# Shared row-sum products, 128-key leftover scores, ten filler products and a new written-out order in a sparse-attention plus rational-MLP kernel

## The chip, the core and the metric

The kernel runs on one NeuronCore of a Trainium2 chip. A core has a matrix engine (PE, with its weight loads shown as PEld), a vector engine (DVE), an activation engine (ACT), a general engine (POOL), and a sync engine (SP) that here only starts transfers. Each engine executes its own instruction list in order; they meet through semaphores. Transfers started from SP and from POOL are carried by the same 16 DMA engines. The metric is the device time of one execution in microseconds; the kernel before took 363.92 us as the median of nine runs (361.21 to 365.72).

## The reference

For 8 batches, 8 heads, 576 positions and head size 64, attention is computed with two masks, and its result goes through a two-layer network with a rational activation:

```python
scores = scale * np.matmul(q, k.transpose(0, 1, 3, 2))
mask_local = (rel >= 0) & (rel < 32)                               # heads 0..3
mask_strided = (rel >= 0) & (pos[None, :] % 32 == pos[:, None] % 32)  # heads 4..7
attn = softmax(np.where(mask, scores, -1e9)); attn_out = np.matmul(attn, v)
x = attn_out.transpose(0, 2, 1, 3).reshape(4608, 512)
h = x @ w_in                                    # 512 -> 2048
g = (a0 + a1*h + a2*h**2 + a3*h**3) / (1 + |b0||h| + |b1|h**2 + 1e-6)
out = g @ w_out                                 # 2048 -> 512
```

## The kernel before

**Stages.** The work is cut into 8 batches of attention and 9 chunks of 512 rows for the network: chunk c < 8 is the first 512 positions of batch c, chunk 8 collects the 64 leftover positions of all batches. For a batch b, `loads(b)` starts the transfers of q, k and v; `scores(b)` makes transposed copies and scores; `attend(b, ...)` makes five output tiles T0 to T4 (T4 is the leftover one); `dense1(c)` is the first layer with the activation; `dense2(c)` the second layer and the store.

**Scores.** R1 transposes the strided heads' k and q on PE into `sT` (for b < TB = 4; later batches use a DMA transpose, step T). R2 and R3 do the same for the local heads (`kL`, `qL`). S and L are the strided and the local scores, each followed by an exponential on ACT into `ES` and `EL`. TL is a DMA transpose of the leftover rows (`tm` to `LT`), X the leftover scores (into `EX`, `EW`). Masks are added by products of `IDN` and `MK`.

**Attend.** A tile is a set of small products into one PSUM pair: 16 local ones (`EL` times `VL`) and 8 strided ones (`ES` times v). For b = 1, 2, 3 (VSB = 4) the strided v lies without a column of ones, so each strided product has a second one with one column, against `ONE`, for the row sum. DVE then takes the reciprocal of the sums (L877) and multiplies (L879) into one of three buffers `XR`; the transpose of `XR` into `XT` is done on PE for b < 2 and by a DMA transpose from SP (L909) after that. Since there are three `XR` buffers, tile n+3 can be written only when the transpose of tile n has been read out: in batch 2, T3 uses the buffer of T0.

**Network.** `dense1` makes eight pairs of 4 x 2 products of 512 columns per chunk (written below as D1.c.f0, f2, ... f14), copied by ACT into `HB` (L975). DVE and ACT evaluate the rational function in steps called d1 to d9 in the code (L989 to L1040; the logarithm and the exponential that make the reciprocal are on ACT, L1013 and L1016). Chunk 0 is cut into groups of 2, 2, 4 and 8 slices, chunk 1 into 4, 4 and 8, so that DVE can begin early. `dense2` is 4 x 8 products for each of two halves (D2.c).

**Order.** Every operation gets a rank from the list `ORDER`, in the sequence in which the program adds operations; each engine's instruction list is its operations sorted by rank. So `ORDER` alone says what stands before what on PE, DVE, ACT, and on the two queues of transfers, SP and POOL. `fill` is a set of NF0 = 20 products of 128 x 512 whose results are not used; they stand on PE among the first operations. The POOL transfers that carry `hw0` wait for the fourth q/k transfer of batch 0 (the q of heads 0 to 3). The transfers of batch b's q and k wait until the transposes of batch b-1 have read their buffers, and those of v until the tiles of the batch before have been computed.

Of the kernel before, what the change touches and what calls it, by code (L numbers as in the profile page):

```python
# [7 lines left out]
BF = dt.bfloat16  # L8
F32 = dt.float32
# [6 lines left out]
def _bf16_bits(x):  # L16
# [7 lines left out]
    5, 7, 13, 9, 15, 103, 38, 43, 45, 55, 20, 46, 171, 85, 2, 0, 42, 68, 79, 63, 61, 69, 65, 82, 70, 59, 76,  # L24
    97, 29, 62, 22, 24, 99, 23, 106, 32, 57, 4, 19, 6, 21, 11, 36, 10, 26, 16, 18, 12, 8, 17, 14, 56, 72,
    66, 51, 37, 110, 141, 145, 30, 41, 44, 49, 50, 33, 52, 35, 27, 28, 54, 87, 90, 71, 80, 96, 100, 25, 31,
    39, 48, 34, 40, 47, 64, 53, 58, 75, 78, 81, 89, 101, 83, 88, 91, 94, 98, 86, 93, 95, 102, 111, 104, 108,
    109, 112, 114, 77, 116, 120, 123, 125, 128, 133, 135, 168, 60, 73, 92, 107, 118, 124, 127, 130, 139,
    136, 117, 132, 121, 126, 84, 74, 105, 67, 131, 137, 3, 1, 192, 198, 182, 173, 113, 138, 140, 143, 144,
    148, 164, 169, 153, 157, 122, 129, 142, 146, 150, 152, 159, 154, 156, 160, 163, 172, 174, 115, 119, 134,  # L30
    147, 151, 183, 187, 158, 161, 166, 170, 208, 215, 167, 176, 155, 165, 185, 188, 191, 224, 234, 195, 201,
    211, 254, 277, 282, 190, 197, 181, 193, 205, 213, 196, 204, 222, 236, 244, 288, 297, 257, 303, 262, 269,
    291, 298, 317, 322, 175, 179, 180, 203, 207, 178, 184, 199, 219, 221, 220, 226, 227, 230, 241, 212, 217,
    218, 223, 246, 162, 209, 216, 233, 231, 240, 253, 260, 263, 149, 186, 194, 202, 239, 235, 200, 245, 247,
    252, 232, 249, 243, 238, 189, 210, 177, 206, 256, 259, 214, 255, 268, 258, 265, 261, 279, 225, 229, 237,
    242, 248, 251, 264, 271, 274, 278, 275, 311, 319, 321, 324, 283, 286, 287, 290, 292, 295, 296, 300, 299,
    304, 305, 308, 307, 315, 316, 318, 329, 369, 375, 384, 250, 266, 267, 273, 281, 289, 306, 313, 327, 314,
    320, 336, 357, 361, 365, 285, 294, 280, 284, 310, 333, 339, 378, 402, 343, 348, 387, 395, 401, 418, 301,
    323, 293, 309, 325, 331, 312, 326, 351, 370, 377, 412, 421, 429, 446, 383, 389, 451, 456, 461, 466, 272,
    228, 276, 270, 347, 344, 350, 338, 349, 341, 353, 355, 342, 302, 332, 335, 360, 359, 382, 379, 367, 364,  # L40
    427, 431, 424, 434, 328, 330, 334, 337, 352, 358, 362, 368, 373, 385, 372, 393, 399, 441, 439, 396, 406,
    407, 411, 420, 425, 426, 430, 432, 435, 438, 444, 442, 449, 450, 453, 462, 489, 492, 496, 340, 346, 345,
    354, 356, 363, 366, 374, 376, 381, 380, 388, 386, 391, 390, 397, 409, 428, 440, 482, 537, 464, 504, 473,
    477, 565, 574, 519, 550, 455, 486, 494, 516, 525, 546, 553, 585, 405, 413, 422, 433, 443, 457, 507, 447,
    454, 459, 467, 472, 531, 509, 371, 394, 404, 436, 410, 417, 392, 400, 414, 415, 419, 398, 423, 408, 468,
    469, 475, 465, 505, 501, 471, 479, 488, 487, 483, 481, 474, 485, 506, 524, 534, 520, 518, 416, 403, 437,
    458, 445, 452, 463, 476, 490, 499, 511, 517, 460, 498, 521, 529, 528, 539, 542, 544, 555, 547, 558, 559,
    570, 564, 569, 571, 575, 573, 581, 583, 586, 589, 601, 602, 605, 470, 480, 484, 491, 503, 512, 532, 543,
    523, 533, 540, 548, 551, 557, 549, 554, 560, 572, 577, 582, 608, 651, 660, 590, 595, 673, 692, 634, 700,
    594, 604, 611, 627, 637, 657, 667, 706, 478, 495, 515, 556, 563, 567, 628, 568, 576, 579, 584, 588, 672,  # L50
    631, 448, 514, 530, 538, 500, 493, 527, 502, 536, 497, 508, 510, 522, 513, 593, 597, 599, 600, 622, 624,
    633, 614, 616, 629, 621, 620, 618, 625, 606, 654, 649, 655, 535, 526, 545, 541, 562, 578, 587, 591, 603,
    617, 623, 630, 552, 580, 638, 648, 646, 662, 664, 665, 668, 669, 674, 675, 677, 680, 684, 685, 689, 688,
    693, 694, 697, 702, 731, 733, 758, 607, 615, 619, 626, 632, 643, 656, 666, 650, 658, 663, 670, 676, 682,
    671, 678, 687, 696, 701, 728, 746, 772, 785, 713, 717, 801, 813, 760, 790, 708, 726, 735, 752, 763, 783,
    792, 822, 592, 598, 613, 641, 686, 766, 764, 691, 698, 703, 709, 718, 820, 810, 561, 566, 652, 659, 640,
    610, 635, 644, 612, 645, 596, 639, 636, 609, 707, 710, 712, 704, 737, 734, 724, 716, 736, 732, 721, 740,
    727, 729, 771, 774, 745, 770, 681, 647, 642, 653, 683, 690, 695, 699, 720, 725, 738, 742, 661, 705, 748,
    753, 757, 775, 779, 780, 784, 786, 789, 791, 805, 794, 798, 799, 803, 804, 808, 814, 816, 824, 864, 871,
    874, 714, 722, 730, 739, 743, 754, 768, 778, 761, 769, 776, 781, 787, 796, 782, 797, 802, 809, 815, 823,  # L60
    870, 858, 877, 830, 834, 885, 901, 897, 905, 832, 840, 845, 865, 873, 881, 887, 916, 723, 750, 795, 800,
    807, 859, 891, 812, 818, 827, 841, 850, 863, 919, 747, 679, 755, 749, 741, 765, 744, 711, 762, 767, 756,
    759, 715, 719, 829, 826, 835, 831, 856, 853, 842, 848, 839, 851, 849, 837, 838, 844, 857, 855, 861, 862,
    773, 777, 751, 793, 806, 811, 817, 821, 825, 828, 833, 846, 788, 819, 852, 866, 868, 878, 880, 886, 889,
    892, 895, 896, 911, 899, 902, 906, 908, 909, 912, 915, 917, 921, 924, 951, 954, 836, 843, 847, 854, 860,
    869, 875, 882, 872, 876, 879, 883, 888, 893, 884, 890, 898, 903, 907, 926, 941, 922, 929, 925, 927, 937,
    962, 946, 953, 914, 931, 934, 940, 944, 952, 960, 965, 867, 894, 900, 904, 910, 957, 920, 913, 918, 923,
    928, 935, 956, 961, 930, 933, 936, 939, 942, 945, 932, 948, 947, 950, 955, 959, 963, 967, 958, 964, 970,
    975, 977, 996, 1002, 986, 1000, 980, 983, 1018, 1022, 1005, 1015, 981, 985, 988, 999, 1003, 1009, 1016,
    1027, 938, 943, 949, 966, 969, 974, 971, 978, 982, 984, 987, 991, 995, 993, 968, 973, 976, 979, 990,  # L70
    994, 972, 989, 997, 1021, 1023, 1040, 1047, 1033, 1037, 1032, 1036, 1042, 1046, 1053, 1058, 1006, 1008,
    1025, 1030, 1035, 1039, 1043, 1050, 1057, 1051, 1055, 1060, 1063, 1067, 1071, 1044, 1054, 1062, 1066,
    1069, 1072, 1079, 1074, 1078, 1085, 1090, 1094, 1097, 1007, 1011, 1019, 1077, 1082, 1086, 1091, 1088,
    1092, 1095, 1098, 1100, 1102, 992, 998, 1001, 1004, 1010, 1013, 1014, 1012, 1017, 1020, 1024, 1026,
    1031, 1028, 1029, 1034, 1038, 1041, 1045, 1048, 1083, 1049, 1052, 1056, 1059, 1075, 1087, 1081, 1061,
    1064, 1065, 1068, 1070, 1073, 1076, 1080, 1084, 1089, 1093, 1096, 1099, 1101, 1103, 1104, 1105, 1106,
    1107, 1110, 1108, 1109, 1112, 1111
# [203 lines left out]
def bass_strided_sparse_attn__then__act_rational_pade_kernel(nc, q, k, v, moe_w_in, moe_w_out, moe_a, moe_b, out):  # L281
# [12 lines left out]
    HL, DA, TB, NF0, VSB = 4, 1, 4, 20, 4  # L294
    PM1, PM2, PAV, PSC = "HHHS", "O", "A", "S"
    VS = 68
    HALF = 0
# [47 lines left out]
    MK = A("MK", [128, 640], BF)  # L345
# [31 lines left out]
    mk = np.tile(half, (2, 1))  # L377
# [236 lines left out]
    def tp(out_ap, l, r):  # L614
        return lambda e: e.matmul(out_ap, l, r, start=True, stop=True, is_transpose=True, skip_group_check=True)  # L615
# [8 lines left out]

    t_free = {"sT": [], "qL": [], "kL": [], "kLl": [], "LT": []}
# [14 lines left out]
    def scores(b, evs=None):  # L640
# [7 lines left out]
        evs = {} if evs is None else evs  # L648
        sets = {"R1": "S", "R2": "S", "R3": "S", "S": "S", "L": "S", "X": "S"}
# [6 lines left out]
        for n, name in enumerate(order):  # L656
# [31 lines left out]
            elif name == "R1":  # L688
                makers = []
                for x, T in ((1, K), (0, Q)):  # L690
                    for gh in range(2):
                        for h in range(4):
                            o = (h * 2 + gh) * 128
                            makers.append(tp(pb[:, x, o:o + 128], T[:, 4 + h, 128 * gh:128 * gh + 128], IDN[:, :]))
# [33 lines left out]
            elif name == "S":  # L728
                makers = quads(ps, 0, 512, M_S, idn8, True)
                for u in range(8):  # L730
                    h, gh = divmod(u, 2)
                    for c in range(2):
                        for j in range(2):
                            makers.append(mm(ps[64 * c:64 * c + 64, j, 64 * u:64 * u + 64],
                                             sT[64 * j:64 * j + 64, 1, h, gh, c:128:2],
                                             sT[64 * j:64 * j + 64, 0, h, gh, c:128:2], False, False))
# [440 lines left out]
```

## Time and profile before

| | |
|---|---|
| nine runs | 361.21 to 365.72 us, median 363.92 us |
| profiled execution | 365.72 us, of which the span from first to last instruction is 363.2 us |
| PE busy | 326.5 us, 90% |
| DVE busy | 314.8 us, 87% |
| ACT busy | 285.4 us, 79% |
| first product of chunk 0's first layer | 31.33 us |
| first product of chunk 2's first layer | 93.29 us |
| last store started | 356.92 us |

Times inside the execution are counted from the start of the span. The page lists busy times by engine, the span in 40 slices, the chain of work that ended last, and groups of instructions by line. Matmuls of the same shape overlap, so where small products are priced, the distance from one group's start to the next group's start is used and not the length of one product.

### The profile page before, as it was taken

Reading aid. Unit: us, or ns where it says so; the run is one execution under the profiler, and the core shown is the slowest. Engines: PE = TensorE matmul, PEld = TensorE weight load, DVE = VectorE, ACT = ScalarE, POOL = GpSimd, SP = SyncE. Lnnn points to the kernel's source line nnn. Section 1 sums busy time; section 2 is a strip of 40 time slices with the busy share of each in tenths; the row PEclk is TensorE's granted clock in tenths of the full one; section 3 lists DMA queues with packets and bytes.
Section 4 is the critical chain, followed back from the end, with each engine's and each line's share of the span. In section 5 each row is a group of like instructions: output and inputs, shape, how many; then the busy total and the mean of one; then the engine's idle time right before and its main releaser. Section 6 shows DMA issues by size and latency. Waiting matters only on the chain.

```text
span 363.2 us, 9072 instructions
## 1 busy us (share of the span) xinstructions
PE 326.5 (90%) x4036; PEld 163.8 (45%) x4036; DVE 314.8 (87%) x281; ACT 285.4 (79%) x234; POOL 150.2 (41%) x216
## 2 busy tenths in 40 slices
PE   0698788994999999999999899999989999999993
PEld 0445446443445554444445344544444454545441
DVE  1372989997996999999977999999989999999992
ACT  2134768895389999898898899999999959999651
POOL 1599195903883079705970991093000000000000
PEclk9879999999699999999999999999999999999998
DMA  8999999699997788996989999494240140222134
GB/s 199 212 151 165 188 90 129 87 132 182 102 158 82 106 82 133 145 180 51 145 98 126 115 99 170 103 90 76 46 101 2 42 109 2 58 58 60 29 87 116
DMA packets 94999, 39.08 MB, mean 108 GB/s; under 512 B 66160, under 2 KB 89904, under 8 KB 94960
## 3 DMA queue, kind: packets, MB, share of 16 engines
q0 software_dynamic: 55104, 16.79, 48.3%
q1 hardware_dynamic: 39856, 21.72, 30.8%
q8 instruction: 31, 0.51, 0.6%
q14 instruction: 8, 0.07, 0.1%
HBM read 36.90 MB, written 9.44 MB: 128 GB/s over the span
## 4 chain that ended last, share of the span: by engine, by line
PE 65%; DMA 10%; DVE 8%; ACT 6%; POOL 5%; SPq 3%; issue 2%; DVEq 0%
PE psO L612 31%; PE psH L612 18%; PE psS L612 9%; PE psA L612 6%; DMA XT<-XR 5%; DMA T<-in_v_dram 2%; DMA qn<-in_q_dram 2%; ACT HB L975 2%; POOL VT L525 2%; POOL tm L483 2%; ACT UU L1013 2%; DVE XR L879 1%; PE psS L615 1%; DVE VL L623 1%; POOL VL L504 1%
## 5 line engine op out<-in xcount | busy, mean ns | idle before, releaser
L612 PE MATMUL psO<-Wout,T 128*128 128x512 bf16 x512 | 117.0, 379 | 2.4 <-ACT OS L1106 2.4
L612 PE MATMUL psH<-XT,Win 128*128 128x512 bf16 x336 | 81.3, 384 | 3.3 <-ACT HB L975 2.3
L1013 ACT ACTIVATE UU<-UU,cst 128x2048 bf16<-128x2048 bf16 (+1 forms) x38 | 72.4, 1908 | 5.0 <-DVE UU L1004 5.0
L612 PEld LDWEIGHTS psO<-Wout,T 128*128 128x128 bf16 x512 | 47.9, 98 | 58.2 <-ACT OS L1106 3.2
L1016 ACT ACTIVATE UU<-UU 128x2048 bf16<-128x2048 bf16 (+1 forms) x38 | 68.7, 1818 | 0.2
L975 ACT ACTIVATE HB<-psH 128x1024 bf16<-128x1024 f32 x48 | 49.1, 1023 | 17.3 <-PE psH L612 17.1
L612 PEld LDWEIGHTS psH<-XT,Win 128*128 128x128 bf16 x336 | 31.0, 97 | 41.1 <-ACT HB L975 3.2
L504 POOL DMA_DIRECT2D VL<-in_v_dram x24 | 20.9, 879 | 59.3 <-PE psA L612 59.2
L1040 DVE TENSOR_TENSOR T<-T,UU 128x4096 bf16<-128x4096 bf16 (+2 forms) x23 | 41.9, 1822 | 0.8 <-ACT UU L1016 0.6
L1004 DVE TENSOR_TENSOR UU<-UU,T 128x4096 bf16<-128x4096 bf16 (+2 forms) x23 | 41.9, 1824 | 0.4
L1030 DVE TENSOR_TENSOR T<-T,HB 128x8192 bf16<-128x8192 bf16 (+3 forms) x17 | 41.0, 2412 | 0.3
L1034 DVE TENSOR_TENSOR T<-T,HB 128x8192 bf16<-128x8192 bf16 (+3 forms) x17 | 41.0, 2410 | 0.2
L879 DVE TENSOR_TENSOR XR<-psA,RC 128x512 bf16<-128x512 f32 (+1 forms) x35 | 22.0, 629 | 6.1 <-DMA XT<-XR 5.1
L483 POOL DMA_DIRECT2D tm<-in_q_dram x32 | 21.5, 676 | 11.4 <-DMA HB<-in_q_dram 10.4
L1001 DVE TENSOR_SCALAR UU<-T,coef 128x4096 bf16<-128x4096 bf16 (+2 forms) x23 | 25.7, 1122 | 0.2
L1023 ACT ACTIVATE T<-HB,coef 128x4096 bf16<-128x4096 bf16 x6 | 22.8, 3799 | 1.7 <-DVE UU L1004 1.5
L525 POOL DMA_DIRECT2D VT<-in_v_dram x32 | 24.1, 780 | 0.0
L1032 DVE TENSOR_SCALAR T<-T,coef 128x8192 bf16<-128x8192 bf16 (+3 forms) x17 | 23.5, 1381 | 0.1
L612 PE MATMUL psO<-XT,Win 128*128 128x512 bf16 x96 | 23.3, 384 | 0.4 <-ACT HB L975 0.4
L1037 DVE TENSOR_SCALAR T<-T,coef 128x8192 bf16<-128x8192 bf16 (+3 forms) x17 | 23.1, 1359 | 0.2
L989 DVE TENSOR_SCALAR T<-HB 128x8192 uint16<-128x8192 uint16 (+3 forms) x17 | 22.1, 1297 | 0.4 <-ACT HB L975 0.4
L483 POOL DMA_DIRECT2D tm<-in_k_dram x32 | 20.3, 636 | 2.9 <-DMA LT<-tm 2.9
(168 smaller groups left out, 444.0 us busy)
## 6 DMA issues: line engine op xcount, KB each, us to landing
out_dram<-OS SPq DMA_DIRECT2D x36, 256.0 KB, 3.6
kn<-in_k_dram POOLq DMA_DIRECT2D x14, 256.0 KB, 5.4
qn<-in_q_dram POOLq DMA_DIRECT2D x14, 256.0 KB, 5.3
Win<-in_moe_w_in_dram POOLq DMA_DIRECT2D x4, 512.0 KB, 7.5
Wout<-in_moe_w_out_dram POOLq DMA_DIRECT2D x1, 2048.0 KB, 21.5
VL<-in_v_dram POOLq DMA_DIRECT2D x24, 72.0 KB, 3.2
HB<-in_k_dram SPq DMA_DIRECT2D x2, 512.0 KB, 7.8
HB<-in_q_dram SPq DMA_DIRECT2D x2, 512.0 KB, 7.1
```

The costliest lines, as they stand in the source:

```text
L483: add("POOL", (lambda e, h=h, r0=r0: e.dma_start(tm[r0:r0 + 16, :].rearrange("x (g y d) -> x y g d", g=4, y=2)[:, h % 2], src[b, h, 512:57 ...
L525: add("POOL", (lambda e, h=h, c=c: e.dma_start(vtp(i)[64 * c:64 * c + 64, h, :, 0:64], v[b, 4 + h, 0:512, :].rearrange("(x c g) d -> c x g ...
L612: return lambda e: e.matmul(out_ap, l, r, start=start, stop=stop, skip_group_check=True)
L879: o3 = add("DVE", (lambda d, rc=rc, x=x, src=src, nh_=nh_: d.tensor_tensor(x[:, 0:64 * nh_].rearrange("x (h d) -> x h d", h=nh_), src[:, : ...
L975: o2 = add("ACT", (lambda a, hd=hd, hs=hs: a.activation(hd, hs, AF.Copy)), [o1, old], ca(1024), key.of("HB"))
L1001: d2 = add("DVE", (lambda d, u=u, t3=t3, sl=sl, HG=HG: d.tensor_scalar(u[:, 0:HG, :], t3[:, sl, :], b1_ap, b0_ap, op0=Alu.mult, op1=Alu.add)),
L1004: d3 = add("DVE", (lambda d, u=u, t3=t3, sl=sl, HG=HG: d.tensor_tensor(u[:, 0:HG, :], u[:, 0:HG, :], t3[:, sl, :], op=Alu.mult)), [d2], ct ...
L1013: ln = add("ACT", (lambda a, u=u, zl=zl: a.activation(u[:, zl, :], u[:, zl, :], AF.Ln, bias=cst[:, 0:1], scale=1.0)), [d3, cons], 0.28 + w ...
L1016: ex.append(add("ACT", (lambda a, u=u, zl=zl: a.activation(u[:, zl, :], u[:, zl, :], AF.Exp, scale=-1.0)), [ln], 0.21 + w * 0.000833, kz + ...
L1030: d5 = add("DVE", (lambda d, hb=hb, t3=t3, g_=g_: d.tensor_tensor(t3[:, g_, :], t3[:, g_, :], hb[:, g_, :], op=Alu.mult)), [d4], ctt(n), k ...
L1034: d7 = add("DVE", (lambda d, hb=hb, t3=t3, g_=g_: d.tensor_tensor(t3[:, g_, :], t3[:, g_, :], hb[:, g_, :], op=Alu.mult)), [d6], ctt(n), k ...
L1040: d9 = add("DVE", (lambda d, t3=t3, u=u, sl=sl, HG=HG: d.tensor_tensor(t3[:, sl, :], t3[:, sl, :], u[:, 0:HG, :], op=Alu.mult)), [d8, ex], ...
```

## The change

It has four parts. First, for b = 1, 2, 3 the one-column products against `ONE` go. Instead tiles T0 and T1 each get four products whose stationary side is all 128 partitions of `ES` (both halves of the strided keys) and whose moving side is a two-column matrix of ones (`ON2`, appended to `MK`): column 64 then holds the sum for the tile itself and column 65 that for tile T+2. The reciprocal of T0 or T1 is taken over 16 numbers into `RG`, that of T2 or T3 only over its four local sums. In T4, eight products of 64 stationary columns take the place of sixteen of 32. Second, for b < 4, R1 uses a permuted identity, so that even and odd positions lie one after the other in `sT`; S reads halves in place of every second column, and X makes 16 products with 128 stationary columns in place of 32 with 64. Third, NF0 goes from 20 to 10. Fourth, `ORDER` is another list.

```diff
-    HL, DA, TB, NF0, VSB = 4, 1, 4, 20, 4
+    HL, DA, TB, NF0, VSB = 4, 1, 4, 10, 4
-    MK = A("MK", [128, 640], BF)
+    MK = A("MK", [128, 642], BF)
+    RG = [A(f"RG{i}", [128, 2, 8], F32) for i in range(2)]
+    ON2 = MK[:, 640:642]
...
+        def half(c):
+            return slice(64 * c, 64 * c + 64) if b < TB else slice(c, 128, 2)
...
-                            makers.append(tp(pb[:, x, o:o + 128], T[:, 4 + h, 128 * gh:128 * gh + 128], IDN[:, :]))
+                            makers.append(tp(pb[:, x, o:o + 128], T[:, 4 + h, 128 * gh:128 * gh + 128],
+                                             IDN.rearrange("x (p c) -> x c p", c=2)))
...
-                                             sT[64 * j:64 * j + 64, 1, h, gh, c:128:2],
-                                             sT[64 * j:64 * j + 64, 0, h, gh, c:128:2], False, False))
+                                             sT[64 * j:64 * j + 64, 1, h, gh, half(c)],
+                                             sT[64 * j:64 * j + 64, 0, h, gh, half(c)], False, False))
...
+                    if b < TB:
+                        for j in range(2):
+                            makers.append(mm(ps[:, j, 64 + 16 * u:80 + 16 * u],
+                                             sT[64 * j:64 * j + 64, 1, h, gh, :],
+                                             LT[64 * j:64 * j + 64, gh, 64 + h:128:4], False, False))
+                        continue
...
+                pair0 = int(0 < b < VSB and T < 2)
-                            makers.append(mm(o_[:, 64:65], w, ONE[vr, :], False, True))
+                if pair0:
+                    deps.append(c_mk)
+                    for h in range(4):
+                        makers.append(mm(pa4[:, 1, h, 64:66], ES[es][:, 2 * h + T, :, :].rearrange("x j q -> x (j q)"),
+                                         ON2, False, True))
...
-                                makers.append(mm(o_[:, 64:65], w, ONE[:, :], False, False))
+                if 0 < b < VSB:
+                    for h in range(4):
+                        for j in range(2):
+                            makers.append(mm(pa4[64:128, 0, h, 64:65],
+                                             EW[es][:, j, 2 * h:2 * h + 2, :].rearrange("x g q -> x (g q)"),
+                                             ONE[:, :], False, False))
...
+            if 0 < b < VSB and T < 4:
+                c2, gh = divmod(T, 2)
+                rc = RG[gh][:, c2, :].rearrange("x (h o) -> x h o", o=1)
+                if c2 == 0:
+                    o2 = add("DVE", (lambda d, gh=gh, src=src: d.reciprocal(
+                        RG[gh].rearrange("x c h -> x h c"), src[:, :, 64:66])), [o1, rg_free[gh]], 0.21, key.of("N"))
+                    rg_ev[gh] = o2
+                else:
+                    o2 = add("DVE", (lambda d, gh=gh, src=src: d.reciprocal(
+                        RG[gh][:, 1:2, 0:4].rearrange("x c h -> x h c"), src[:, 0:4, 64:65])),
+                        [o1, rg_ev[gh]], 0.19, key.of("N"))
```

What the two lists mean where the prediction speaks of them (A2.T0 is tile T0 of batch 2; "t" its transpose on PE; sT1 is the copy of batch 1's transposes; mul and rcp are DVE's multiply and reciprocal):

```
SP, first transfers (k0, q0: heads 4-7 of batch 0; k1, q1: heads 0-3; v: heads 0-3; w0, w1: v of heads 4-7)
before  k0 IDN q0 MK v a q1 k1 v cst w1 b v w0 v
after   w0 q0 IDN q1 MK b cst k0 a k1 v v v v w1
PE, from batch 1's R1
before  S1.R1 D1.0.f2 S0.X D1.0.f0 A0.T4 S1.R2 S1.R3 S1.L D1.0.f6 S1.S D1.0.f4 A1.T0 A1.T1 D1.0.f10 f8 f14 ...
after   S0.X A0.T1t A0.T3t S1.R1 D1.0.f2 f0 f6 f4 A0.T4 S1.R3 S1.R2 f10 S1.S S1.L f8 A1.T1 A1.T0 f14 ...
PE, around batch 3's scores
before  ... D1.1.f12 S3.R1 A2.T4 S3.R2 D1.2.f0 D1.2.f2 S3.R3 D1.2.f4 S3.S D1.2.f6 S3.L D1.2.f8 ...
after   ... D1.1.f12 S3.R2 A2.T4 S3.R3 S3.S D1.2.f0 D1.2.f2 S3.L D1.2.f4 D1.2.f6 D1.2.f8 ...
DVE
before  ... A0.T4.rcp, d1 of f2, A0.T4.mul, sT1, d1 of f0, ...; VW memset of batch 1 at rank 171
after   ... sT1, d1 d2 d3 of f2, d1-d5 of f0, d4 of f2, A0.T4.rcp, ...; VW memset of batch 1 at rank 64
DVE, between A2.T0.mul and A2.T3.mul, and POOL
before  A2.T3.mul at rank 316; w_out's transfer at rank 279, after ten tm, two VT, four VW and four q/k transfers
after   A2.T3.mul at rank 315, behind four more steps (d8 of chunk 0, d5, d6 of chunk 1, sT3), d1 of chunk 1's second group behind it;
        w_out's transfer at rank 260
POOL, first weights of the first layer
before  Win0 before most of batch 0's tm, Win1 after batch 1's v and q/k, Win2 and Win3 after batch 1's tm
after   Win0, Win1 after batch 0's tm and three of batch 1's q/k, Win2 and Win3 among batch 1's tm
```

## The prediction

> **What bounds the kernel now.** I read the busy times of a few long stretches first, to see which engine is full where. Columns: stretch, length, then busy time and count of PE, weight loads, DVE, ACT, POOL, then PE's granted clock, DMA share, GB/s.
>
> ```profile
> 0.00:36.00 36.00, 21.94 (x390) 12.99 (x394) 13.49 (x29) 9.80 (x13) 24.59 (x42) 0.91 1.17 181
> 36.00:81.00 45.00, 38.48 (x797) 21.56 (x796) 43.04 (x63) 37.84 (x37) 24.36 (x36) 1.00 1.09 128
> 81.00:93.00 12.00, 6.51 (x151) 4.31 (x148) 8.85 (x9) 6.45 (x8) 5.65 (x9) 0.91 1.31 173
> 93.00:357.00 264.00, 259.51 (x2708) 124.95 (x2708) 248.76 (x181) 230.71 (x178) 95.64 (x131) 0.99 0.68 90
> ```
>
> Four stages with four limits: transfers up to 36 us, DVE from 36 to 81 (2.0 us idle in 45), a hole at 81 to 93 in which PE idles 5.5 us and DVE 3.1, and then 264 us in which PE idles 4.5. So the end is the moment at which PE leaves the hole, plus the PE work that is left then. The chain that ended last shows what makes the hole.
>
> ```profile
> 72.01 0.69 DVE XR L879
> 72.73 11.40 DMA XT<-XR
> 84.94 8.30 DMA XT<-XR
> 93.29 3.60 PE psH L612 x8
> ```
>
> Tile T0 of batch 2 is transposed by DMA in 11.40 us; T3 shares its buffer and waits for that; T3's transpose takes 8.30; then chunk 2 begins, its first group at half speed (3.60 against 1.73 for such a group further on). Over all 24 of these transposes the median landing is 4.3 us, so these two stand in a queue. In front of them are three q/k transfers and w_out (2 MB, issued at 70.91, landed 21.5 us later). The waits show why w_out is that late and what holds DVE before.
>
> ```profile
> DVE RC L877 <- PE psA L612: 15.0, 10, 5.9
> ...
> DVE XR L879 <- DMA XT<-XR: 5.1, 2, 3.1
> ```
>
> ```profile
> POOL T L533 <- DVE T L419: 8.2, 1, 8.2
> ...
> POOL qn L474 <- PE psS L615: 4.0, 1, 4.0
> ```
>
> DVE's longest wait (5.9 us, 30.5 to 36.4) is the reciprocal of A0.T4, with chunk 0's first step right behind it in the list. POOL stands 8.2 us (37.5 to 45.7) for a memset that DVE has at rank 171, then 4.0 us for S2.R1, and issues without a break from 59.1 to w_out. Between 63 and 72 us the DMA share is only 0.65.
>
> **What the Trainium skill says.** "TensorE: Matmul & The Clock Gate" (Part 1, the HAM clock gate): the array runs at half rate until it has been busy for about 3.4 us. The trace agrees: fillers average 470 ns against 377 for the same shape later, and the first group after the hole takes 3.60 us. The same page (Part 2, Weight-path perf modes) says weight loads of 128 columns have a faster path; here they take 98 ns and those of 64 columns 108, which agrees. "DMA: Bandwidth & Descriptors" (Issuing engines are not separate DMA queues): transfers from SP and POOL share the same 16 engines and interleave; the 11.40 us above is that.
>
> **The change part by part.** Sums are against the profiled execution, 365.72 us with a span of 363.2 (2.5 us around it).
>
> *Products.* Starts of groups in the timeline price them. In batch 2's T0 the 16 strided and one-column products run from 71.30 to 71.65, 0.35 us; batch 0's 8 without sums take 0.24 (24.88 to 25.12). So removal saves 0.11 us on each of 12 tiles, 1.3. Added on 6 tiles: four full-array products, whose loads I bound by 56 ns (the step of R1's 128 x 128 products, 0.45 us for 8) and 98 ns (a load in full): 0.22 to 0.39 each, 1.3 to 2.4. T4: 0.52 becomes 0.35 plus 8 x 30 ns (the step of the 64-column products of R2), +0.07 three times. X: 32 products in 0.26 us; sixteen with 128 columns cost 0.13 if they keep the 8 ns step and 0.78 if two row halves of 98 ns loads alternate; I take 0.35, four times +0.1. Reciprocals stay 0.18 to 0.21. Contiguous `sT` and the strided identity cost nothing: strided moving operands already run at 376 ns per 512 columns, contiguous ones at 379. Together +0.8 us of PE (bounds -0.5 to +3.5); only batch 3's share is behind the hole, +0.2 (-0.2 to +0.9). Before it PE has 5 us of slack.
>
> *Ten fillers fewer.* At 0.22 to 0.47 us each they stood where PE waited for data: 0. What they may keep up is the clock. If chunk 0 starts cold, one group takes 3.6 instead of 1.9: up to +1.7 us, taken as 0 and kept for the range.
>
> *Order, start.* SP's first transfers are the same 3.3 MB (198 and 214 GB/s in the first two 9 us), so the last still lands at about 19.8. Now the last is w1, not v. The three v casts (3.72 us) can start 256 KB / 0.21 MB per us = 1.2 us earlier, at 18.6, and the w cast (0.97) follows: A0.T0 at 23.4 in place of 24.64. From there: 0.6 to the first reciprocal, four times 0.9 on DVE, one 0.41 copy, 0.4 and 0.6 for the last transpose and its ACT copy, 0.9 for S1.R1, some overlapping: 6.3 against 6.7 us. D1.0.f2 starts at 29.7 (31.33), -1.6. The first k lands later than before (eighth issue, not first) but R1 to L then still end before the casts do.
>
> *Order, DVE.* A0.T4 no longer precedes chunk 0. Its first step can run when HB is copied: 29.7 + 1.9 + 1.0 = 32.6 (36.52), and sT1 (1.21), done behind the wait before, is done by then. DVE is 5.1 us ahead. Up to A2.T3's multiply the new list holds 1.28 + 1.22 + 0.75 + 1.21 more and 0.69 less, +3.8. Walking the list I find stalls of about 2 us more than before, most at sT2, behind a 1.99 us logarithm on ACT. Before, the multiply could have run at 81.1 and ran at 84.22; now 81.1 - 5.1 + 3.8 + 2.0 = 81.8.
>
> *Order, POOL.* The memset is early, so the 8.2 us wait goes. Next on POOL is v of batch 2, which waits for A0.T4 at about 37; then batch 2's small transfers from about 45 (they ran at 59.9 and later), and w_out behind S2.R3 (62.84, less some 5): issued at about 59, landed near 81. T3's transpose then meets a free queue: I take 5.5 us, between the 4.3 median and the 8.3 seen. Landing: 81.8 + 0.7 + 5.5 = 88.0, plus 0.5 for issue. **PE resumes at 88.5 in place of 93.3, -4.8.** Batch 3's v waits for A2.T4 and then had 8.6 us to spare before A3.T0; both move together.
>
> *Order, behind the hole.* S3.R3 and S3.S (0.57 and 0.60) are now ahead of D1.2.f0, in the hole: -1.2.
>
> Sum: -4.8 - 1.2 + 0.2 = -5.8. I give back 1.6: PE idles only 4.5 us behind the hole, but DVE is full there in places (49.54 of 50 us from 200 to 250), and a back half in another order need not fit as well. **-4.2 us**: 361.5 on the profiled execution's scale. That one was the slowest of nine, 1.8 above the median, so 363.9 - 4.2 = 359.7.
>
> **Rivals.** *The hole stays.* w_out early collides with batch 2's and 3's other loads instead, and T0's and T3's transposes again take 11 and 8 us: resume near 92, gain 1 to 1.5, about 362.8. For: the DMA share is above 1 nearly everywhere up to 93. Against: 63 to 72 us is idle. *The start is blocked by weights (slower).* D1.0.f6 becomes PE's third group, at 33.3 us (41.44 before), and needs Win1, which I expect issued near 22 us and landed near 30 to 33, by the 7.5 us median of the four. If it lands later, PE stops with f4, A0.T4 and batch 1's scores behind it, and POOL's v of batch 2 behind A0.T4. Each microsecond late comes off the lead: none is left when it lands at 37.5, and beyond 39.3 the kernel is slower by over 0.5%: 366 to 368. For: 18 to 36 us is where the DMA engines are fullest (1.29 to 1.36). *The back half gives it back*: PE waits 3 to 6 us more for DVE or transposes behind 93, 363 to 366.5. Against: its PE list is nearly the old one. *The hole closes*: T3's transpose at 4.3, no extra stalls, nothing given back: 356.
>
> **How the numbers follow.** Within 0.5% (1.8 us) is about what a measurement of this kernel can tell from no change. Main case 0.48 (358 to 361.7), hole closes 0.12, hole stays 0.18 (362 to 364.5), weights late 0.12, back half 0.10 (half of it slower). Faster: 0.48 + 0.12 + 0.03 of the third = 0.63; slower: 0.12 + 0.05 + 0.02 for a cold start on top of the third case = 0.19; same 0.18. Range 355.5 to 366, leaving out about 0.05 below and 0.12 above. It has cases of both signs; the main case's own is 358 to 361.7.
>
> **What would show it.** Right: chunk 0's first product near 29.7 us; DVE's first step near 32.6; no 8 us wait of POOL for the memset; w_out issued near 59; T3's transpose under 6 us; chunk 2's first product near 88.5. Wrong: a PE wait for Win at D1.0.f6, fillers' absence as a granted clock near 0.5 at 30 us, transposes of 8 us or more, or PE waits of over 6 us behind the hole. T0 and T1 of batches 1 to 3 should take PE no less time than before.

## The result, and the profile after

The changed kernel takes 366.2 us (median of 16 executions, 362.53 to 373.24) against 363.92 us before (53 executions): a ratio of 1.0096 with an interval of [1.0067, 1.0125], so it is slower by about 1%. The profiled execution took 367.98 us, again 1.8 us above its median, so the two profiles differ by what the medians differ by (2.26 and 2.28 us). The ratio leaves out executions over 1.5% above the fastest of their kernel (both profiled ones here, and twelve of the 19 of new_20_fillers below), which the medians keep.

The same four stretches as in the prediction, in the changed kernel (columns as there):

```profile
0.00:36.00 36.00, 21.98 (x341) 14.27 (x342) 14.66 (x32) 9.32 (x11) 26.62 (x44) 0.86 1.30 185
36.00:81.00 45.00, 40.61 (x723) 22.48 (x721) 40.73 (x57) 35.18 (x36) 22.10 (x33) 0.92 1.18 158
81.00:93.00 12.00, 9.26 (x197) 5.82 (x198) 11.53 (x14) 10.89 (x11) 2.25 (x4) 1.00 0.25 40
93.00:357.00 264.00, 255.01 (x2599) 123.47 (x2598) 246.28 (x179) 228.63 (x175) 104.45 (x137) 0.99 0.68 90
```

The hole between 81 and 93 us is filled: PE is busy 9.26 us there (6.51 before), DVE 11.53 (8.85), and the DMA engines are nearly free (0.25 against 1.31). But that bought almost nothing: chunk 2's first product starts at 92.80 us (93.29 before). Two other lines got worse. From 36 to 81 us PE is busier (40.61 against 38.48) at a clock of 0.92 (1.00 before), and DVE, which had been full there, idles 4.3 us. From 93 to 357 us PE idles 9.0 us (4.5 before). The waits name what PE stands for (columns: total, times and longest, in us; of the first line 2.4 us lie behind 93 us, the others wholly):

```profile
PE psH L612 <- ACT HB L1014: 4.4, 5, 1.8
...
PE psA L612 <- DMA VL<-VL: 2.8, 1, 2.8
PE psA L612 <- DMA VT<-in_v_dram: 2.7, 1, 2.7
```

Neither of the two transfer waits was in the kernel before. The first is A3.T0 at 110.57 us (v of batch 3, local heads), the second A6.T0 at 221.54 us (v of batch 6, strided heads). Both come back in the profile of a shorter execution with the same list (new_20_fillers below: 1.7 and 3.3 us). The chain that ended last runs through the first of them (columns: start, length, what):

```profile
88.26 0.99 PE psS L612 x16
89.26 1.06 PE psA L612 x48
90.75 0.74 POOL VL L504
91.50 2.27 POOL tm L483 x4
...
97.02 2.80 POOL tm L483 x2
99.82 2.64 DMA tm<-in_q_dram
102.48 1.19 SPq L688
103.71 0.61 SPq L510
104.36 6.16 DMA VL<-VL
110.57 0.73 PE psA L612 x28
```

A2.T4 (89.26) frees the v buffer; POOL, which stood 26.5 us for it, then issues the four VL transfers mixed with ten leftover q/k transfers (`tm`) of the same batch. The last VL is issued at 100.48 and lands at 103.15. SP first issues the leftover transpose (L688), which waited for the last of the ten until 102.46, and then the two shifted copies of v; the later one lands at 110.53. In the kernel before it landed at 104.33, 7.35 us before A3.T0 needed it.

The granted clock of PE, read in the stretches in which it fell, first of the kernel after, then the first two of before:

```profile
22.70:33.00 10.30, 9.74 (x170) 7.03 (x171) 4.67 (x11) 1.85 (x4) 10.30 (x17) 0.50 1.47 162
60.30:67.10 6.80, 6.73 (x80) 4.05 (x80) 6.76 (x7) 2.52 (x4) 3.53 (x4) 0.50 1.25 160
111.50:114.90 3.40, 3.40 (x42) 1.47 (x28) 3.12 (x4) 3.40 (x3) 3.40 (x6) 0.50 0.79 93
```

```profile
22.70:33.00 10.30, 8.74 (x149) 4.81 (x146) 6.36 (x14) 2.23 (x4) 10.30 (x16) 1.00 1.36 139
60.30:67.10 6.80, 6.21 (x138) 3.81 (x139) 6.77 (x8) 6.55 (x6) 6.80 (x12) 1.00 0.70 86
```

Between its last early filler (20.20) and A0.T0 (23.26) PE idled 3.06 us (0.61 before A0.T0 in the kernel before, whose fillers ran until 24.03). The clock halved at 22.7 us and stayed so for 10.3 us, through A0's tiles, S1.R1 (1.71 us to the next group against 0.89) and up to the first product of chunk 0, which started at 32.86 in place of 31.33. It halved again at 60.3, behind waits of 0.36 and 1.12 us, and at 111.5, right behind the wait at A3.T0.

### The profile page after: what moved, and what is told of

It reads as the page before. It is cut to its first block, busy times and chain, and to the rows that moved or that the text cites. A ratio compares the mean times of both kernels' runs of the same rounds, so it can differ in the third digit from the quotient of the medians.

```text
span 365.8 us, 8727 instructions
## 1 busy us (share of the span) xinstructions
PE 329.1 (90%) x3866; PEld 166.8 (46%) x3866; DVE 314.6 (86%) x281; ACT 285.2 (78%) x234; POOL 155.4 (42%) x216
## 4 chain that ended last, share of the span: by engine, by line
PE 68%; ACT 11%; POOL 7%; DMA 5%; SPq 3%; DVE 2%; issue 1%
PE psO L612 30%; PE psH L612 16%; PE psS L612 12%; PE psA L612 7%; POOL tm L483 3%; ACT HB L1014 3%; ACT UU L1055 3%; ACT UU L1052 2%; DMA T<-in_v_dram 2%; DMA VL<-VL 2%; POOL VL L504 2%; PE psS L615 1%; POOL VT L525 1%; SPq L559 1%; DMA VT<-in_v_dram 1%; ACT T L1062 1%
## 5 line engine op out<-in xcount | busy, mean ns | idle before, releaser
L612 PE MATMUL psO<-Wout,T 128*128 128x512 bf16 x512 | 118.5, 383 | 0.6 <-ACT OS L1145 0.6
L612 PE MATMUL psH<-XT,Win 128*128 128x512 bf16 x336 | 79.6, 378 | 4.5 <-ACT HB L1014 4.4
L525 POOL DMA_DIRECT2D VT<-in_v_dram x32 | 25.6, 838 | 6.7 <-PE psA L612 6.7
L1145 ACT ACTIVATE OS<-psO 128x1024 f32<-128x1024 f32 x16 | 16.4, 1023 | 14.2 <-PE psO L612 14.2
L612 PE MATMUL psO<-XT,Win 128*128 128x512 bf16 x96 | 24.3, 398 | 0.2 <-ACT HB L1014 0.2
L1076 DVE TENSOR_SCALAR T<-T,coef 128x8192 bf16<-128x8192 bf16 (+3 forms) x17 | 22.9, 1346 | 0.3
L483 POOL DMA_DIRECT2D tm<-in_q_dram x32 | 19.9, 628 | 6.6 <-DMA HB<-in_q_dram 6.6
L483 POOL DMA_DIRECT2D tm<-in_k_dram x32 | 22.6, 710 | 0.0
```

Source lines behind the costliest of these rows:

```text
L483: add("POOL", (lambda e, h=h, r0=r0: e.dma_start(tm[r0:r0 + 16, :].rearrange("x (g y d) -> x y g d", g=4, y=2)[:, h % 2], src[b, h, 512:57 ...
L525: add("POOL", (lambda e, h=h, c=c: e.dma_start(vtp(i)[64 * c:64 * c + 64, h, :, 0:64], v[b, 4 + h, 0:512, :].rearrange("(x c g) d -> c x g ...
L612: return lambda e: e.matmul(out_ap, l, r, start=start, stop=stop, skip_group_check=True)
```

## The experiments

Three causes were held against each other: **clock** (fewer fillers and new gaps halve PE's clock), **waits** (v comes late for A3.T0 and A6.T0), and **products** (the new sums cost PE). Ranks are entries of `ORDER`; "new" and "old" are the changed list and the list before. Each run was timed beside the kernel before.

| run | list | products | fillers | us, median | before beside it | ratio |
|---|---|---|---|---|---|---|
| the change itself | new | new | 10 | 366.2 | 363.92 | 1.0096 [1.0067, 1.0125] |
| new_20_fillers | new | new | 20 | 367.89 | 363.38 | 1.0021 [0.9982, 1.0060] |
| old_10_fillers | old | old | 10 | 365.79 | 363.38 | 1.0073 [1.0050, 1.0097] |
| old_order_new_products | old | new | 20 | 361.74 | 363.38 | 0.9983 [0.9953, 1.0012] |
| new_order_old_products | new | old | 20 | 364.17 | 363.38 | 1.0011 [0.9978, 1.0044] |
| new_v_early | new, v moved | new | 10 | 361.71 | 363.5 | 0.9952 [0.9927, 0.9976] |
| new_v_early_34_fillers | new, v moved | new | 34 | 360.13 | 363.5 | 0.9926 [0.9900, 0.9952] |
| old_order_mended | old, 4 places | new | 20 | 360.76 | 363.5 | 0.9947 [0.9918, 0.9975] |
| new_34_fillers | new | new | 34 | 365.51 | 363.5 | 1.0039 [1.0009, 1.0069] |
| new_v3_early | new, batch 3's v | new | 10 | 365.11 | 362.79 | 1.0063 [1.0032, 1.0094] |
| new_v6_early | new, batch 6's v | new | 10 | 364.3 | 362.79 | 1.0046 [1.0020, 1.0071] |
| old_products_v_early | new, v moved | old | 34 | 359.44 | 362.79 | 0.9923 [0.9893, 0.9953] |
| new_v_early_34_f0_first | new, v moved, D1.2.f0 first | new | 34 | 360.04 | 362.79 | 0.9945 [0.9912, 0.9978] |

### The change taken apart

```diff
 # changed kernel, ten more fillers between the last early one and A0.T0
-    HL, DA, TB, NF0, VSB = 4, 1, 4, 10, 4
+    HL, DA, TB, NF0, VSB = 4, 1, 4, 20, 4
+    # ranks of the ten: 58.05, 58.10, ... 58.50 (A0.T0 has 74)
```

> The changed kernel with ten more filler products, all placed on PE between the last early filler and A0.T0, where PE idled 3.06 us (20.20 to 23.26) in the changed kernel. Clock theory (the missing fillers let PE's clock fall to half at 22.7 us, and 10.3 us at half clock put chunk 0 back): the granted clock stays at 1.0 from about 19 to at least 55 us, S1.R1 takes about 1.06 us in place of 1.91, D1.0.f2 starts near 30.0 in place of 32.86, and the time is 2 to 4 us below the changed kernel's, 362 to 364. Order theory (the loss is in the new list, above all in the waits for v at A3.T0 and A6.T0, and fillers are worth nothing): within 0.7 us of the changed kernel, 365.5 to 367. Products theory (the new sums cost PE the time): also no change.

The median is 367.89 us, the ratio 1.0021. These disagree: seven executions took 361.65 to 366.46 us, and the ratio rests on them; twelve took 367.11 to 369.69. In the profiled one (365.75 us) the first half clock was gone, D1.0.f2 started at 29.15 and DVE's first step at 32.13, as the clock theory says. But the clock halved from 47.4 to 54.2 instead, behind 2.37 us in which PE stood among the first products of A1.T0 (the profile shows nothing that it waited for), and both transfer waits were there (1.7 and 3.3 us). So the early start was lost again before the end. What separates the twelve from the seven was not profiled and stays open.

```diff
 # kernel before, without the fillers at ranks 57 59 61 62 63 65 68 69 70 76
-    HL, DA, TB, NF0, VSB = 4, 1, 4, 20, 4
+    HL, DA, TB, NF0, VSB = 4, 1, 4, 10, 4
```

> The kernel before without the nine fillers between S0.L and A0.T0 and the one behind A0.T0; nothing else is changed. Clock theory: PE idles some 3 us before A0.T0, the half clock that ends at 22.6 us in the kernel before goes on to about 30 or 33, D1.0.f2 starts 2 to 3 us later (about 33.5 to 34) and the time rises by 1 to 3 us, to 365 to 367. Order or products theory, and the prediction's own step on the fillers (0 us): no change, 363.5 to 364.5.

The time rises by 2.4 us in the median, 0.73% in the ratio, with an interval well above 1. Nothing but fillers was removed. In the profile PE idles 4.63 us before A0.T0, and the clock is at half from 21.6 us:

```profile
15.00:21.60 6.60, 2.36 (x120) 1.75 (x116) 4.56 (x10) 2.96 (x3) 6.60 (x10) 1.00 1.31 173
21.60:28.40 6.80, 5.89 (x112) 3.66 (x112) 4.24 (x10) 0.60 (x1) 6.80 (x10) 0.50 1.35 138
```

The kernel before has a half clock of the same length, but earlier:

```profile
15.75:22.58 6.83, 5.59 (x124) 3.73 (x125) 4.50 (x11) 2.19 (x3) 6.82 (x11) 0.50 1.28 165
```

So without the ten fillers the half clock is not longer; it lies behind A0.T0 and no longer ahead of it, where A0.T0 still has to wait for v. From A0.T0 to D1.0.f2 it takes 8.2 us in place of 6.7. D1.0.f2 itself came at 30.72, not at 33.5 to 34 as expected, because A0.T0 came at 22.51 (24.64 in the profile of before). Nor do 20 fillers always keep that stretch at full clock: in old_order_new_products below it is at half from 23.9 to 27.4. Where the rest of the 2.4 us is lost was not traced. Removing the ten fillers alone, in the old list, thus costs about as much as the whole change (0.73% against 0.96%, with overlapping intervals); that it does so through the clock is read from this profile and was not tested apart.

```diff
 # changed code with the list before and NF0 = 20
```

> The new products (shared sums, 128-key leftover scores, halves in place of every second column) with the old list and 20 fillers. Prediction's step on the products: +0.8 us (-0.5 to +3.5), little of it behind the hole, so 363.9 to 364.7. Products theory: 366 or more. Clock and order theories: no change, within 0.7 us of the kernel before.

361.74 us, ratio 0.9983 with 1 inside the interval: in the old list the products theory falls. The mirror run has the old code with the new list and 20 fillers:

> The old products with the new list and 20 fillers (the ten extra ones placed as in the run with the changed kernel and 20 fillers). Clock theory: as that run, about 0.5 us lower for the cheaper products, 361.5 to 363.5. Order theory: about 365.5, since the list alone loses the time. Products theory: at or below the kernel before, 360 to 363.9, and well below the changed kernel with 20 fillers.

364.17 us, ratio 1.0011: no measurable difference from the kernel before, nor, by the ratio, from the same list with the new products (1.0021). The list alone, with its fillers, brings nothing, and the transfer waits are in it too: PE stood 0.85 us at A3.T0 and 2.05 at A6.T0 (there the profile names a DVE step, but the last v transfer landed at 217.39 and PE went on 0.13 us later, as in the changed kernel). The medians say less: 364.17 against 367.89 with the new products, and none of these 14 executions took more than 366.52 us, where twelve of those 19 did. So a cost of the new products in this list is not excluded; no run has the new list, the old products and ten fillers.

### The transfers of v

```diff
 # POOL: ten leftover q/k transfers of batch 3, directly behind w_out (260)
-    ranks 327, 330, 331, 334, 335, 341, 343, 349, 351, 353
+    ranks 260.05, 260.10, ... 260.50
 # SP: leftover transpose (TL) of batch 3
-    rank 367
+    rank 304.5
 # POOL: last three strided v transfers of batch 6, ahead of batch 7's leftover q/k
-    ranks 745, 748, 754
+    ranks 720.1, 720.2, 720.3
```

> The changed kernel with ten fillers, only transfers reordered: the ten leftover q/k transfers of batch 3 right behind w_out (where POOL stood from 64.3 to 90.8 us for A2.T4), the leftover transpose of batch 3 ahead of T2's transpose on SP, and the last three strided v transfers of batch 6 ahead of the leftover q/k transfers of batch 7. Waits theory (the back half loses the time because v comes late for A3.T0 and A6.T0): the PE waits of 2.83 us at A3.T0 and 2.73 us at A6.T0 go, with them the 3.4 us at half clock at 111.5, and the time falls by 3 to 6 us, to 360.5 to 363.5. Rival (DVE and ACT are full there, so the waits come back elsewhere): at most 1.5 us less than the changed kernel, 365 or more. Clock theory: the half clock at 22.7 and 60.3 stays, so chunk 2's first product stays near 92.8.

361.71 us: 4.5 us less than the changed kernel, ratio 0.9952 against 1.0096 (1.44% of 363.5 is 5.2 us), with intervals far apart. Both transfer waits are gone; the longest PE wait for a DMA is the start's. That the front had no part in it is seen in the same profile:

```profile
0.00:36.00 36.00, 21.17 (x344) 13.85 (x349) 16.11 (x34) 10.13 (x12) 27.09 (x44) 0.86 1.22 193
36.00:81.00 45.00, 38.63 (x727) 21.34 (x732) 40.18 (x56) 34.62 (x38) 27.96 (x42) 0.92 1.17 155
```

The clocks up to 81 us are those of the changed kernel (0.86, 0.92), and chunk 2 starts at 92.23 (92.80); yet A3.T0 starts at 107.11 in place of 110.57 and the last group of products at 351.17 in place of 358.23. The two halves of the edit were also run alone:

> Only batch 3's half of new_v_early (its leftover q/k transfers behind w_out, its leftover transpose earlier on SP), ten fillers. If the wait at A3.T0 and the half clock behind it carry the loss: 1.5 to 4 us below the changed kernel (366.2), 362 to 364.7, and the wait at A6.T0 stays near 2.7 us. If A6.T0's carries it: no change, 365.5 to 366.5.

> Only batch 6's half of new_v_early (three strided v transfers ahead of batch 7's leftover q/k), ten fillers. If the waits add up: 1 to 3.5 us below the changed kernel, 362.7 to 365.2, with the 2.8 us wait at A3.T0 still there. If A3.T0's wait carries the loss alone: no change, 365.5 to 366.5.

365.11 and 364.3 us, ratios 1.0063 and 1.0046. Each lies 0.3% and 0.5% below the change itself, and each keeps the other's wait (2.8 us for VT with batch 3's half, 1.9 us for VL with batch 6's). Both intervals overlap that of the change, so only the two halves together are shown to gain. In ratios the parts sum to 0.83%, the whole is 1.44%; with intervals of 0.3% on each the difference is not shown to be real.

### Fillers once more, with and without the waits

```diff
 # ten fillers before A0.T0, nine between D1.0.f8 and A1.T1, five between S2.R2 and S2.R3
+    MID.append([e])              # batch 1: exponential of S
+    MID.append([e1, e2])         # batch 1: exponentials of X
...
+    for evm, nm in zip(MID, (9, 5)):
+        for _ in range(nm):
+            add("PE", (lambda e: e.matmul(PS["A"][:, 1, :], IDN[:, :], MK[:, 0:512], start=True, stop=True,
+                                          skip_group_check=True)), [c_idn, c_mk, evm], 0.216, 9100.0)
```

> The changed kernel with the 24 extra fillers of new_v_early_34_fillers and its own transfers. Clock theory: no half clock between 20 and 85 us, chunk 2's first product near 90, 2 to 4 us below the changed kernel, 362.5 to 364. Waits theory: the waits at A3.T0 and A6.T0 take it back, since v's arrival is tied to A2.T4 and to POOL's list: no more than 1.5 us below the changed kernel, 365 or more.

365.51 us, ratio 1.0039: better than the change by 0.57%, with intervals that just overlap, and still slower than before. In this execution PE idled 2.69 us before A0.T0 all the same, and the clock was at half from 23.2 to 30.0 us; it was full from there to 91. No wait at A3.T0 shows in this execution. The one at A6.T0 stays, and behind it the clock halves for a further 3.4 us:

```profile
PE psA L620 <- DMA VT<-in_v_dram: 2.8, 1, 2.8
```

```profile
217.80:221.20 3.40, 3.11 (x30) 1.52 (x32) 0.90 (x2) 2.23 (x2) 0.54 (x2) 0.50 1.34 221
```

> The run new_v_early with 24 more fillers: ten before A0.T0, nine between D1.0.f8 and A1.T1 (PE idled 2.37 us there in the run with 20 fillers), five between S2.R2 and S2.R3 (1.12 us idle). Clock theory: no half clock between 20 and 85 us, chunk 2's first product near 90, and 1.5 to 3 us less than new_v_early. Rival (from 70 us on the front is set by ACT, whose copies and logarithms PE waits for in its list order): chunk 2's first product moves by less than 1 us against the run with 20 fillers (91.16), and the time by less than 1.5 us.

360.13 us, ratio 0.9926. The two profiles with 34 fillers run together up to A5.T4 (195.84 and 195.98) and part at A6.T0: D1.6.f0 starts at 236.77 with the wait and at 233.28 without, so this one wait, with its 3.4 us at half clock, is worth 3.5 us. Against new_v_early the fillers bring 1.6 us in the median, but the intervals overlap. The clock in the front is full in this execution:

```profile
20.00:91.00 71.00, 58.54 (x1072) 33.67 (x1082) 58.77 (x86) 48.53 (x51) 44.44 (x68) 1.00 1.20 145
```

(From 91.3 to 94.8 it is at half again, over chunk 2's first groups.) And chunk 2's first product still starts at 92.2. So the half clock does not set the end of the front; the chain of the same profile shows what does:

```profile
82.61 1.80 ACT UU L1068
84.41 0.92 ACT HB L1027
85.33 0.05 issue
85.38 1.47 PE psH L621 x6
...
88.32 1.02 ACT kL L631
89.34 0.92 ACT HB L1027
90.26 0.93 ACT qL L631
91.18 0.04 issue
91.22 1.00 PE psS L621 x36
```

PE and ACT hand the work back and forth: D1.1.f12 (85.38) waits for a copy that ACT makes behind an exponential, S3.S (91.22) for the copy of `qL`. T3's transpose had landed at 89.57. The next edit lets chunk 2 go first:

```diff
 # PE: D1.2.f0 ahead of S3.S
-    rank 336
+    rank 332.5
```

> new_v_early_34_fillers with one more move: D1.2.f0 ahead of S3.S on PE. It tests the prediction's step that S3.R3 and S3.S come for nothing in the hole. If S3.S holds chunk 2 up there (PE waits 1.2 us for ACT's copy of qL in front of it, while T3's transpose has landed 2 us before): chunk 2's first product moves from 92.2 to about 90.2 and the time falls by 0.8 to 1.5 us, to 358.6 to 359.3. If S3.S only fills time: no change within 0.6 us, or a loss since the scores come later.

Chunk 2's first product moves to 89.85, 2.3 us earlier, and the time does not: 360.04 us, ratio 0.9945 against 0.9926. A start of chunk 2 that is 2 us earlier makes no kernel here that these runs can tell to be shorter. The last run puts the old products into the mended list:

> new_v_early_34_fillers with the old products (two products for each strided value tile of batches 1 to 3 with one-column sums, 64-key leftover scores). Prediction's step on the products (+0.8 us for the new ones, +0.2 behind the front): 359.3 to 360.1, against 360.1 with the new ones. Products theory (the new ones cost more in the new list than in the old, as 367.9 against 364.2 with 20 fillers suggests): 357 to 358.5. If the new products save time, as 361.7 against 363.4 with the old list suggests: 361 to 362.5.

359.44 us, ratio 0.9923 against 0.9926. The products make no difference that these runs can tell, in the old list or in this one. With either products the mended list takes 0.7% less than the kernel before.

### The old list, mended by the prediction's own steps

```diff
-    memset that POOL waits for: rank 171;  strided q of batch 3: 228;  w_out: 279
+    111.5;  268.5;  269.0
-    ten leftover q/k transfers of batch 3: ranks 302, 338, ... 355
+    279.05 ... 279.50
```

> The new products with the old list and 20 fillers, changed in four places: the memset that POOL stood for from 37 to 45 us is early on DVE, the strided q of batch 3 goes behind batch 2's leftover transfers, w_out directly behind these, and batch 3's leftover q/k transfers behind w_out. Prediction's steps on the memset and w_out: w_out is issued near 58 to 60 in place of 68.7, T3's transpose takes under 6 us in place of 8.5 to 9.7, the hole before D1.2.f0 closes by 2 to 3 us, so 358.5 to 360 against 361.7 for the same products with the old list. Rival (the hole only moves to the next wait): 361 to 362.5.

360.76 us, ratio 0.9947; the same products with the plain old list had 0.9983, so a gain of 0.4% is likely but the intervals overlap. w_out was issued at 60.8 us in place of 68.7 and landed at 81.0. But T3's transpose still took 7.9 us (under 6 was expected), and chunk 2 started at 89.22 (89.58 with the plain old list). The hole moved rather than closed: chunk 2 no longer waits for T3's transpose, but PE stands 3.0 us in front of S3.R1, for ACT:

```profile
PE psS L622 <- ACT HB L1021: 3.0, 1, 3.0
```

## Why the prediction was wrong

It forecast 359.7 us (355.5 to 366.0); the result is 366.2. Two terms of its sum failed: the -4.8 us for PE's return, of which -0.5 came, and the back half, where it gave back 1.6 us and late transfers of v cost 5.2 by the ratio. The second turned the gain into a loss, for with these transfers mended the same list is 0.5% faster than before. By its own steps:

- **The back half: this step failed.** The prediction wrote that batch 3's v "waits for A2.T4 and then had 8.6 us to spare before A3.T0; both move together", and so put it at nothing; the 1.6 us that it gave back was reasoned from DVE. To spare were 7.35 us, and the two moved apart. The shifted v landed 6.20 us later (110.53 against 104.33): POOL could begin 3.40 us later because A2.T4 came later (90.75 against 87.35), its issues up to the last VL took 1.18 longer, that transfer landed 0.93 faster, and from there to the landing of the shifted copies, with the leftover transpose ahead of them on SP, it took 2.55 longer. And A3.T0 could have started 3.94 us earlier (107.74 against 111.68). Together 10.1 us, more than the 7.35 to spare: a wait of 2.8. At A6.T0 the same happened through three transfers that the new list puts behind ten of batch 7's: landed at 221.41, before at 211.31. With both mended the kernel gains 5.2 us by the ratio. The rival "the back half gives it back" came, with its 363 to 366.5 us and PE waits of 3 to 6 us (4.5 more idle time), but by transfers that it did not name (it named DVE and the DMA transposes).
- **PE resumes at 88.5: this step failed too.** It resumed at 92.80. The transposes were no longer the limit (T3 landed at 89.8); the limit was the exchange with ACT, which the prediction did not walk. The rival "the hole stays" had the time right (near 92), but through transposes of 11 and 8 us. S3.R3 and S3.S did go into the hole, but with a wait of 1.2 us for ACT in front of S3.S. Even undoing that gained no time that can be told, so the premise that the end is the moment at which PE leaves the hole plus the work left did not hold in this list.
- **Ten fillers fewer: the term was mis-sized.** Taken as 0, with +1.7 us as its bound; measured alone in the old list it is +2.4 us (ratio 1.0073). The prediction priced one cold group. In the changed kernel the clock stayed at half for 10.3 us, over everything that ran there. In the new list the effect is not settled as well: 0.6% with the waits in place (34 fillers), 0.3% when they are mended, both with overlapping intervals.
- **Start.** A0.T0 came at 23.26 as forecast (23.4), but that is luck and not shown to come from the list: other runs of the old list had it at 22.5 and 22.9, and the 24.64 of the profiled execution of before was a late one. D1.0.f2 came at 32.86, not 29.7: half clock. With v mended and 34 fillers it started at 30.46, behind a wait of 1.8 us for the first weights (Win0, landed at 30.3). The weights rival had looked at Win1 for D1.0.f6; in the changed kernel nothing waited for it.
- **DVE.** The first step ran at 35.91 (forecast 32.6), A2.T3's multiply at 86.80 (81.8). At full clock (34 fillers, v mended) they are at 33.4 and 85.8. So the clock explains most of the first miss and little of the second: a lead on DVE is worth nothing where DVE then waits for PE's list. In that run it idles 2.4 us for A1.T0, in which PE itself stood 1.8 us without a wait that the profile shows, and 1.1 us for S1.X; the prediction had put all new stalls at 2 us.
- **POOL.** Right: the memset's wait is gone, w_out was issued at 62.5 (59) and landed at 80.06 (81), and T3's transpose took 2.3 us (5.5 forecast, 8.30 before).
- **Products.** Right in the old list and in the mended one, where the runs show no difference; with the plain new list and 20 fillers it stays open, as said above. In the profiles at full clock, from a group's start to the next start or to its end where PE then idles, batch 2 takes: T0 0.59 (0.58 before), T1 0.66 (0.58), T2 0.48 (0.58), T3 0.55 (0.65), T4 1.11 (0.95), X 0.81 (0.69), together +0.17 us a batch and some +0.6 with batch 0's X (forecast +0.8).

With v mended and more fillers than before the new list takes 360.1 us, near the 359.7 that was forecast. That is no confirmation: the front's gain did not come, and what makes up for it was not traced. One part can be seen without the added fillers: in the profile of before the clock is at half until 97.7, which from chunk 2's start at 93.29 on costs about 2 us (an estimate, half of the 4.4 us), and in that of new_v_early it is full there. The prediction had read chunk 2's slow first group but put nothing in its sum for it.

## What to carry to other kernels

When a list is rearranged, walk each buffer that is filled by a transfer from its release to its use, on both sides: what makes the release later and what makes the use earlier are subtracted from the same slack, and so is every transfer that stands ahead in the queue. Products that only keep the array busy are part of the schedule: before removing one, ask which gap it covers and price half the clock over all that runs for the next microseconds, not over one group. An earlier start of one stage counts only as far as the next engine in the chain is not already the one that sets it.

## What was not expected of the hardware

- *The clock comes back later than busy time suggests.* The changes of the clock lie at 22.7, 33.0, 60.3, 67.1, 111.5 and 114.9 us: apart by 10.3, 27.3, 6.8, 44.4 and 3.4 us, which are 3, 8, 2, 13 and 1 steps of 3.41 to 3.43 us. This agrees with the Trainium skill, "TensorE: Matmul & The Clock Gate" (Part 1, the HAM clock gate), which tells of a free-running window of 3.4 us. The section also says that one busy window brings the full clock back. Here it did not: from 26.1 to 29.6 us PE was busy 3.50 of 3.50 us, and the clock stayed at half until 33.0. What ran there were tiles of many small products, eight transposes of 128 x 128 and two fillers; which of them does not count was not tested:

```profile
26.10:29.60 3.50, 3.50 (x78) 2.44 (x74) 2.50 (x7) 0.00 (x0) 3.50 (x6) 0.50 1.24 194
```

- *A window need not be idle to lose the clock.* From 56.9 to 60.3 us PE was busy 1.99 of 3.40 us and the clock halved at its end; in the kernel before it was busy 1.88 of 3.50 us from 36.2 to 39.7 and kept it. Busy time alone does not decide; that the kind of product counts was not tested.
- *Copies inside the core can take as long as a larger transfer beside them.* The two shifted copies of v (136 and 153 KB, issued at 103.71 and 104.36) took 6.6 and 6.2 us (4.4 and 4.3 in the kernel before), and the leftover transpose of 102.48 took 7.6, all landing between 110.06 and 110.53, while a 256 KB q transfer issued at 102.45 landed at 109.88. That it held them up was only argued from the times.
